# Turning the last 128 output columns four tiles at a time, with rows loaded by quarters of the contraction

## The chip, the cores and the metric

The kernel runs on one core of one Trainium2 chip. The metric is the device time of one execution in microseconds (us). The engines are TensorE (PE; its weight loads are shown apart as PEld), VectorE (DVE), ScalarE (ACT), GpSimd (POOL) and SyncE (SP). Transfers are issued by SP, ACT and POOL, each of which works through its queue in order.

## The reference

One block of a transformer: attention with a cached key and value store, gated by a feed-forward network.

```python
xn = layernorm(x)                                  # x: 2048 rows of 640
q  = (xn @ wq) -> 32 heads of 192
p  = softmax(q @ k^T * 192 ** -0.5)                # 2048 cached keys a head
s  = concat_heads(p @ v) @ wo                      # wo: 6144 x 640
ffn = (silu(xn @ w1) * (xn @ w3)) @ w2             # 640 -> 1536 -> 640
out = x + s * silu(ffn)
```

All inputs and the output are bfloat16, sums are float32.

## The kernel before, in words

The 2048 rows are 16 tiles of 128 (`NQT`), or 4 blocks of 512 (`NQB`). The attention over 32 heads comes first and takes the largest part of the time. Its normalized result is stored to four DRAM buffers `o_scr`, one for each block, of 512 rows and 6144 columns. Then comes the feed-forward part (`ffn_out` for each block, lines 919 to 937), which leaves the gate in SBUF, and at the end the output projection with `wo`, which is the stage that the change touches.

In the projection the contraction runs over 6144 = 48 pieces of 128 (`OC`). `wo_sb` holds all of `wo`. The rows come back from `o_scr` transposed (a transposing transfer on SP's queue), so that `oT` holds piece k of the contraction on the partitions. The 640 output columns are done in two ways:

- The first 512 (`WIDE`): `oT` is the stationary operand and `wo_sb` streams 512 columns (`rows_product`, line 873; 48 matmuls a tile).
- The last 128: for the first 14 tiles (`TURNED`) the product is turned. The 128 columns of `wo_sb` are stationary and the rows stream, 256 of them, a pair of tiles at once (`turned_product`, line 882; 48 matmuls a pair). The sum then has columns on partitions and rows along the free axis. The gate `gT` and the input `xT` for it are held in the same turned form, and the result is turned back by a transposing transfer (`store_turned`, line 889) and stored. Tiles 14 and 15 do the last 128 columns as 48 more matmuls of 128 columns (`output_tile`, line 900).

A pair of tiles is loaded by two transposing transfers of 128 whole rows (`load_pair`, line 859) into one of two pools, `otp` and `otq`. Pair 0 is loaded under the feed-forward part, with `xT` behind it (line 944). `otq` lies where the feed-forward weights were, so pair 1 is loaded when those are free. Pair n + 2 is issued when pair n has been used. After each sum VectorE does two steps (`gated_sum`, lines 867 and 868): sum times gate, plus x; ACT issues the store of a tile (line 974) and of the turned columns (line 890). The last tile's stores are issued by SP (line 905), and the wide one waits until the store ahead of it is done (the manual dependency on `acc["out"]`).

PSUM has two pools here: `ps_st` with two buffers of two banks, and `ps_o` with two more (`ob0`, `ob1`). `tail_ps`, used by the feed-forward part, hands them out in turn.

The engines' queues run in the order in which the program is written here (`pin` keeps it); no scheduler moves instructions.

Of the kernel before, what the change touches and what calls it, by code (L numbers as in the profile page):

```python
# [11 lines left out]
BF16 = mybir.dt.bfloat16  # L12
F32 = mybir.dt.float32
I32 = mybir.dt.int32

P = 128
# [8 lines left out]
def _pieces(n, maxw=512):  # L25
    k = -(-n // maxw)
    w = -(-n // k)
    return [(c, min(c + w, n)) for c in range(0, n, w)]


def _kernel_impl(ctx, tc, A_x, A_k_cache, A_v_cache, A_wq, A_wo, B_w1, B_w3, B_w2, out):
    nc = tc.nc
    _, SQ, D = A_x.shape
    _, H, SK, dh = A_k_cache.shape
# [4 lines left out]
    NQT = SQ // P  # L39
    NQB = SQ // 512  # L40
# [4 lines left out]
    OC = HD // P  # L45
# [129 lines left out]
    with ExitStack() as actx:  # L175
# [643 lines left out]
        def tail_ps(name):  # L819
            turn[0] += 1  # L820
            if turn[0] % 2:
                return ps_st.tile([P, 1024], F32, tag="st2", name=name)
            return ps_o.tile([P, 2, 512], F32, tag=f"ob{(turn[0] // 2 + 1) % 2}", name=name)[:].rearrange("p t c -> p (t c)")
# [18 lines left out]
    wo_sb = wop.tile([P, OC, D], BF16, name="wo_sb")  # L842
    gp = ctx.enter_context(tc.tile_pool(name="gp", bufs=1))
    WIDE = 512
    TURNED = NQT - 2
    g_all = gp.tile([P, NQT, WIDE], BF16, name="g_all")
    gT = gp.tile([P, TURNED * P], BF16, name="gT")
    g_last = gp.tile([P, NQT - TURNED, D - WIDE], BF16, name="g_last")
# [1 line left out]
    nc.gpsimd.dma_start(out=wo_sb[:], in_=A_wo.rearrange("(k p) d -> p k d", p=P))  # L850
    flag_i = const.tile([P, 1], I32, name="flag_i")

    def load_pair(pools, n):
        dsb, otp = pools[0], pools[1 + n % 2]
        rows = slice(2 * n * P, 2 * (n + 1) * P)
        oT = otp.tile([P, 2, OC, P], BF16, tag="oT", name="oT")
        for j in range(2):
            i = 2 * n + j
            pin(nc.sync.dma_start_transpose(out=oT[:, j, :, :], in_=o_scr[i // 4][(i % 4) * P:(i % 4 + 1) * P, :]))
        xt = dsb.tile([P, 2, D], BF16, tag="xt", name="xt")  # L860
        nc.gpsimd.dma_start(out=xt[:], in_=x2[rows, :].rearrange("(t p) d -> p t d", p=P))
        return oT, xt

    def gated_sum(pools, ps, g, x, to):
        w = ps.shape[-1]
        tmp = pools[0].tile([P, 512], F32, tag="tmp", name="tmp")
        pin(nc.vector.scalar_tensor_tensor(out=tmp[:, 0:w], in0=ps, scalar=0.25, in1=g, op0=ALU.mult, op1=ALU.mult))
        acc["sum"] = pin(nc.vector.tensor_tensor(out=to, in0=tmp[:, 0:w], in1=x, op=ALU.add))

    def rows_product(pools, i, oT, xt):  # L870
        ps = ps_st.tile([P, 1024], F32, tag="st2", name="ps_s")[:, 0:WIDE]
        for k in range(OC):
            pin(nc.tensor.matmul(ps, lhsT=oT[:, i % 2, k, :], rhs=wo_sb[:, k, 0:WIDE], start=(k == 0), stop=(k == OC - 1)))  # L873
        res = pools[0].tile([P, D], BF16, tag="res", name="res")
        gated_sum(pools, ps, g_all[:, i, :], xt[:, i % 2, 0:WIDE], res[:, 0:WIDE])
        return res

    def turned_product(pools, n, oT):
        cols = slice(2 * n * P, 2 * (n + 1) * P)
        ps = ps_o.tile([P, 2, 512], F32, tag=f"ob{n % 2}", name="ps_t")[:, 0, 0:2 * P]  # L880
        for k in range(OC):
            pin(nc.tensor.matmul(ps, lhsT=wo_sb[:, k, WIDE:D], rhs=oT[:, :, k, :], start=(k == 0), stop=(k == OC - 1)))  # L882
        resT = pools[0].tile([P, 2 * P], BF16, tag="resT", name="resT")
        gated_sum(pools, ps, gT[:, cols], xT[:, cols], resT[:])
        return resT

    def store_turned(pools, n, resT):
        back = pools[0].tile([P, 2, P], BF16, tag="back", name="back")
        pin(nc.sync.dma_start_transpose(out=back[:], in_=resT[:]))
        nc.scalar.dma_start(out=out2[2 * n * P:2 * (n + 1) * P, WIDE:D].rearrange("(t p) d -> p t d", p=P), in_=back[:])  # L890

    def output_tile(pools, i, oT, xt):
        split = i == NQT - 1
        to = nc.sync if split else nc.scalar
        cuts = ((0, WIDE), (WIDE, D))
        ps_s = [ps_st.tile([P, 1024], F32, tag="st2", name="ps_s") for _ in range(2 if split else 1)]
        pieces = [(ps_s[-pi if split else 0][:, pi * 512:pi * 512 + c1 - c0], c0, c1) for pi, (c0, c1) in enumerate(cuts)]
        order = [(k, q) for q in pieces for k in range(OC)] if split else [(k, q) for k in range(OC) for q in pieces]
        for k, (ps, c0, c1) in order:
            pin(nc.tensor.matmul(ps, lhsT=oT[:, i % 2, k, :], rhs=wo_sb[:, k, c0:c1], start=(k == 0), stop=(k == OC - 1)))  # L900
        res = pools[0].tile([P, D], BF16, tag="res", name="res")
        for ps, c0, c1 in pieces:
            g = g_last[:, i - TURNED, :] if c0 else g_all[:, i, :]
            gated_sum(pools, ps, g, xt[:, i % 2, c0:c1], res[:, c0:c1])
            stored = to.dma_start(out=out2[i * P:(i + 1) * P, c0:c1], in_=res[:, c0:c1])
            if split and c0 == 0:
                tc.add_manual_dep(stored.ins, acc["out"].ins.name,
                                  mybir.DependencyInfo(mybir.DependencyClass.Sync, mybir.DependencyReason.DATA),
                                  reason="the tiles ahead are stored ahead")
            acc["out"] = stored  # L910

    def ffn_gate(ps, to):
        w = ps.shape[-1]
# [25 lines left out]
    with ExitStack() as dctx:  # L939
        dsb = dctx.enter_context(tc.tile_pool(name="dsb", bufs=3))  # L940
        pools = [dsb, dctx.enter_context(tc.tile_pool(name="otp", bufs=1))]
        with tc.issue_after(acc["store"].ins):
            pairs = [load_pair(pools, 0)]
            pin(nc.sync.dma_start_transpose(out=xT[:], in_=x2[0:TURNED * P, WIDE:D]))
        for qb in range(NQB):
            if qb + 1 < NQB:
                for fl in range(1 if qb == 0 else 0, FC - FCP):
                    ffn_hidden(qb + 1, fl, tail_ps("ps_gu"))()
            ffn_out(qb)
            if qb + 2 < NQB:  # L950
                load_hT(qb + 2)
            if qb == 0:
                worst = fsb.tile([P, 1], F32, tag="worst", name="worst")
                pin(nc.vector.tensor_reduce(out=worst[:], in_=rl_all[:], axis=AX.X, op=ALU.max))
                low_sum = fsb.tile([P, 1], F32, tag="low_sum", name="low_sum")
                pin(nc.vector.tensor_scalar(out=low_sum[:], in0=worst[:], scalar1=RL_MAX, scalar2=None, op0=ALU.is_gt))
                gap = fsb.tile([P, 1], F32, tag="gap", name="gap")
                pin(nc.vector.tensor_reduce(out=gap[:], in_=gaps[:], axis=AX.X, op=ALU.max))
                bad = fsb.tile([P, 1], BF16, tag="bad", name="bad")
                pin(nc.vector.scalar_tensor_tensor(out=bad[:], in0=gap[:], scalar=GAP_MAX, in1=low_sum[:], op0=ALU.is_gt,  # L960
                                                   op1=ALU.add))
            if qb == 1:
                ps_b = ps_st.tile([P, 1024], F32, tag="st2", name="ps_b")
                pin(nc.tensor.matmul(ps_b[:, 0:1], lhsT=ones_bf[:], rhs=bad[:], start=True, stop=True))
                pin(nc.vector.tensor_copy(out=flag_i[:], in_=ps_b[:, 0:1]))
        fwctx.close()
        pools.append(dctx.enter_context(tc.tile_pool(name="otq", bufs=1, side="right")))
        pairs.append(load_pair(pools, 1))
        for n in range(TURNED // 2):
            oT, xt = pairs.pop(0)  # L970
            for i in range(2 * n, 2 * n + 2):
                res = rows_product(pools, i, oT, xt)
                for c0, c1 in _pieces(WIDE, WIDE if i < TURNED - 4 else WIDE // 2):
                    nc.scalar.dma_start(out=out2[i * P:(i + 1) * P, c0:c1], in_=res[:, c0:c1])
            resT = turned_product(pools, n, oT)
            if n + 2 < NQT // 2:
                pairs.append(load_pair(pools, n + 2))
            store_turned(pools, n, resT)
        oT, xt = pairs.pop(0)
        output_tile(pools, NQT - 2, oT, xt)  # L980
        with tc.block():
            tc.mark_branch_hint_location("redo", "LikelyTaken", (mybir.EngineType.PE,))
            output_tile(pools, NQT - 1, oT, xt)
            wait = pin(nc.tensor.nop())
            tc.add_manual_dep(wait.ins, acc["sum"].ins.name,
                              mybir.DependencyInfo(mybir.DependencyClass.Sync, mybir.DependencyReason.DATA),
                              reason="what follows the jump is fetched behind the last rows")
# [158 lines left out]
```

## Time and profile before

| | us |
|---|---|
| median of 3 runs | 1934.65 |
| lowest and highest run | 1933.1, 1934.7 |
| the profiled execution | 1933.35 |
| its span, first to last instruction | 1931.8 |
| of it: attention and what goes before, to about | 1645 |
| feed-forward part | 1645 to 1720.6 |
| output projection | 1720.6 to the end |

A trace holds one execution. Its times are counted from the start of the span; 1.55 us of the execution lie outside it. A matmul's length in a timeline includes its way through the array, so the cost of one matmul in a stream is read from start to start, not from its length. A transfer has two figures: how long its issue holds the queue, and the time from issue to landing.

### The profile page before, as it was taken

The numbers are of one execution on the slowest core, as the hardware profiler recorded it, in microseconds if no ns is written. First come the engines' busy times: TensorE is split into PE (matmuls) and PEld (weight loads), VectorE is DVE, ScalarE is ACT, GpSimd is POOL, SyncE is SP. The second block draws the span as 40 slices with busy tenths as digits, with TensorE's granted clock in tenths as the row PEclk, the third lists the DMA queues.
The fourth block names the chain that finished last, engine by engine and source line by source line (L and its number), as shares of the span: only waits on it lengthen the run. The fifth ranks groups of instructions, "written<-read, shape, count | busy, mean of one in ns | idle before, by whom it ended". The sixth has DMA issues, their size and how long they took to land.

```text
span 1931.8 us, 59549 instructions
## 1 busy us (share of the span) xinstructions
PE 1925.3 (100%) x26799; PEld 1301.5 (67%) x26823; DVE 953.1 (49%) x1804; ACT 1275.9 (66%) x1285; POOL 446.3 (23%) x755
## 2 busy tenths in 40 slices
PE   9999999999999999999999999999999999999999
PEld 6666666666666667777777776666777777445555
DVE  7765545554545554545555555555554544421111
ACT  7777777777777777777777777777777777210000
POOL 2432222222222222223222222222222210000000
PEclk9999999999999999999999999999999999999999
DMA  8422213131212222232422222212121102947652
GB/s 170 94 71 50 72 41 79 41 80 42 63 39 59 49 63 52 58 77 71 104 55 66 50 71 50 71 42 79 42 80 39 34 10 75 276 102 158 141 137 54
DMA packets 333861, 145.32 MB, mean 75 GB/s; under 512 B 284992, under 2 KB 327424, under 8 KB 333600
## 3 DMA queue, kind: packets, MB, share of 16 engines
q1 hardware_dynamic: 318992, 113.30, 25.2%
q0 software_dynamic: 7744, 23.60, 4.3%
q10 hardware_dynamic: 6864, 4.56, 0.8%
q8 instruction: 211, 3.46, 0.8%
q14 instruction: 50, 0.41, 0.1%
HBM read 56.23 MB, written 31.98 MB: 46 GB/s over the span
## 4 chain that ended last, share of the span: by engine, by line
PE 99%; DMA 0%; DVE 0%; issue 0%; SPq 0%
PE obank L529 35%; PE st L489 34%; PE ps L331 14%; PE ps_s L873 7%; PE ps_f L926 2%; PE ps_t L882 2%; PE ps_s L900 1%; PE ps_gu L315 1%; PE ps_gu L331 1%; PE ps_f L936 0%; DMA x_all<-in_A_x_dram 0%; DVE st L237 0%; PE ps_f L928 0%; PE pst L262 0%; PE pq L315 0%
## 5 line engine op out<-in xcount | busy, mean ns | idle before, releaser
L496 ACT ACTIVATE pT<-st,nb 128x1024 bf16<-128x1024 f32 x960 | 1068.6, 1113 | 327.6 <-PE st L489 323.6
L529 PEld LDWEIGHTS <-pT 64*128 64x128 bf16 x16384 | 725.2, 94 | 230.8 <-ACT pT L496 0.4
L529 PE MATMUL obank<-vt,pT 64*128 64x193 bf16 x16384 | 858.0, 243 | 0.0
L505 DVE TENSOR_REDUCE osum<-obank 128x386 f32<-128x772 f32 x256 | 234.3, 957 | 639.9 <-PE obank L529 639.8
L489 PE MATMUL st<-qF,KT 64*128 64x512 bf16 x1024 | 385.0, 376 | 0.0
L489 PE MATMUL st<-qD,KT 64*128 64x512 bf16 x1024 | 385.0, 376 | 0.0
L489 PE MATMUL st<-qS,KT 64*128 64x512 bf16 x1024 | 384.9, 376 | 0.0
L489 PE MATMUL st<-qS,KS 64*128 64x512 bf16 x1024 | 384.9, 376 | 0.0
L489 PE MATMUL st<-qA,KS 64*128 64x512 bf16 x1024 | 384.9, 376 | 0.0
L489 PE MATMUL st<-qA,KT 64*128 64x512 bf16 x1024 | 384.8, 376 | 0.0
L489 PEld LDWEIGHTS <-KT 64*128 64x128 bf16 x4096 | 293.9, 94 | 130.8 <-issue 0.8
L331 PE MATMUL ps<-xnT,w 64*128 64x512 bf16 (+1 forms) x2540 | 314.5, 374 | 0.0
L365 POOL COPY qS<-qA 64x512 bf16<-64x512 bf16 x254 | 157.3, 619 | 564.4 <-ACT qA L375 555.6
L331 PEld LDWEIGHTS <-w 64*128 64x128 bf16 x2540 | 128.2, 94 | 113.1
L489 PEld LDWEIGHTS <-KS 64*128 64x128 bf16 x2048 | 173.4, 94 | 7.5 <-issue 0.2
L512 DVE TENSOR_TENSOR ostage<-osum,rl_all 128x384 bf16<-128x384 f32 x256 | 142.9, 558 | 8.9
L873 PE MATMUL ps_s<-wo_sb,oT 128*128 128x512 bf16 x658 | 145.4, 379 | 0.7
L154 POOL COPY KS<-KT 64x1024 bf16<-64x1024 bf16 (+1 forms) x68 | 68.3, 1004 | 235.1 <-DMA KT<-in_A_k_cache_dram 217.7
L108 POOL DMA_DIRECT2D w<-in_A_wq_dram x60 | 52.9, 882 | 289.5 <-PE ps L331 289.3
L376 DVE CAST qF<-ps 128x512 bf16<-128x512 f32 x120 | 83.0, 692 | 72.5 <-ACT qA L375 72.5
L873 PEld LDWEIGHTS <-oT 128*128 128x128 bf16 x672 | 65.7, 98 | 77.8
L359 DVE TENSOR_REDUCE st<-qA 128x1 f32<-128x512 bf16 (+1 forms) x130 | 87.4, 672 | 4.8 <-ACT qA L375 4.7
(111 smaller groups left out, 1110.8 us busy)
## 6 DMA issues: line engine op xcount, KB each, us to landing
o_scr<-ostage SPq DMA_DIRECT2D x64, 384.0 KB, 2.8
vt<-in_A_v_cache_dram SPq DMA_DIRECT2D x60, 384.0 KB, 5.0
wo_sb<-in_A_wo_dram POOLq DMA_DIRECT2D x1, 7680.0 KB, 31.6
w<-in_A_wq_dram POOLq DMA_DIRECT2D x30, 160.0 KB, 3.6
hT_scr<-hblk SPq DMA_DIRECT2D x16, 256.0 KB, 3.1
xt<-in_A_x_dram POOLq DMA_DIRECT2D x8, 320.0 KB, 3.4
w<-in_B_w_dram POOLq DMA_DIRECT2D x30, 80.0 KB, 2.6
w<-in_A_wq_dram POOLq DMA_DIRECT2D x30, 80.0 KB, 3.0
```

Source lines behind the costliest of these rows:

```text
L108: return lambda eng: keep(eng.dma_start(out=w[:, :, c0:c1], in_=src[:, s0:s0 + c1 - c0].rearrange("(c p) d -> p c d", p=P)))
L154: return [keep(nc.gpsimd.tensor_copy(out=KS[ROWS[r], c0:c1], in_=ks[ROWS[1 - r], 2 * r, c0:c1])) for r in range(2)]
L331: mm = pin(nc.tensor.matmul(out[:, t * 512 + t0 * P:t * 512 + (t0 + step) * P], lhsT=ws[t][ROWS[r], c, :], rhs=rows_of(qb, c, ROWS[r], t0, ...
L359: pin(nc.vector.tensor_reduce(out=hd["st"][r, 2 + s, qb:qb + 1], in_=src[r, qb * 512:qb * 512 + n], axis=AX.X, op=ALU.max, apply_absolute_ ...
L365: return [lambda t=t: keep(copy(out=hd["qS"][ROWS[t], qs], in_=hd["qA"][ROWS[1 - t], qs])) for t in range(2)]
L376: pin(cast(out=hd["qF"][:, qs], in_=ps[:, 512:1024]))
L489: pin(nc.tensor.matmul(st2[:, t * 512:(t + 1) * 512], lhsT=k[ROWS[t]], rhs=q[ROWS[t], qs], start=(s == 0), stop=(s == 2)))
L496: pin(nc.scalar.activation(out=pT2[:, c0:c1], in_=st2[:, c0:c1], func=ACT.Exp, scale=SCALE, bias=nb))
L505: pin(nc.vector.tensor_reduce(out=osum[:], in_=ob[:].rearrange("p t (j c) -> p j c t", j=2)[:, :, 0:DH + 1, :], axis=AX.X, op=ALU.add))
L512: pin(nc.vector.tensor_tensor(out=ostage[:, b * 2:b * 2 + 2, hg * DH:(hg + 1) * DH], in0=osum[:, :, 0:DH], in1=rl.unsqueeze(2).to_broadcas ...
L529: pin(nc.tensor.matmul(acc["o"][b][:, r, j * 256:j * 256 + DH + 1], lhsT=pT2[ROWS[r], t * 512 + i * P:t * 512 + (i + 1) * P], rhs=vt[ROWS[ ...
L873: pin(nc.tensor.matmul(ps, lhsT=oT[:, i % 2, k, :], rhs=wo_sb[:, k, 0:WIDE], start=(k == 0), stop=(k == OC - 1)))
```

## The change

The projection goes by blocks of four tiles instead of pairs. The stationary 128 columns of `wo` now meet 512 rows in one matmul; `TURNED` grows from 14 to 15 tiles, so the last block has three tiles in this form (384 rows) and only tile 15 is done in the other way. A block is loaded by quarters of the contraction: 12 of the 48 pieces for up to 512 rows, in one transposing transfer (`load_quarter`). There are four buffers for quarters, two in each of the two pools; quarters 0 and 1 are loaded under the feed-forward part, and quarter n + 4 is issued when quarter n has been used. Tile 15 has a load of its own (`load_last`), in the shape of before.

Within a quarter each of the four tiles adds its 12 pieces, then the turned product its 12, so that four wide sums and a turned one stay open over the block: three PSUM buffers of two banks, two wide sums in one buffer, taken by `tail_ps`. VectorE's steps and the stores of all four tiles come in the block's fourth quarter. Tiles from the sixth on are stored in two pieces (before: from the eleventh on). In the feed-forward part the turned product of the last block takes three tiles instead of two, and tile 14's matmuls of 128 columns go.

```diff
-    TURNED = NQT - 2
+    TURNED = NQT - 1
+    QUARTER = OC // 4
...
-    def load_pair(pools, n):
-        dsb, otp = pools[0], pools[1 + n % 2]
-        rows = slice(2 * n * P, 2 * (n + 1) * P)
-        oT = otp.tile([P, 2, OC, P], BF16, tag="oT", name="oT")
-        for j in range(2):
-            i = 2 * n + j
-            pin(nc.sync.dma_start_transpose(out=oT[:, j, :, :], in_=o_scr[i // 4][(i % 4) * P:(i % 4 + 1) * P, :]))
...
+    def load_quarter(pools, n):
+        q, k0 = n // 4, n % 4 * QUARTER
+        w = min(4, TURNED - 4 * q) * P
+        oT = pools[1 + n % 4 // 2].tile([P, QUARTER, 512], BF16, tag=f"oT{n % 2}", name="oT")
+        pin(nc.sync.dma_start_transpose(out=oT[:, :, 0:w], in_=o_scr[q][0:w, k0 * P:(k0 + QUARTER) * P]))
+        return oT
+
+    def load_last(pools):
+        oT = pools[1].tile([P, OC, P], BF16, tag="oT0", name="oT_last")
+        pin(nc.sync.dma_start_transpose(out=oT[:], in_=o_scr[NQB - 1][512 - P:512, :]))
+        return oT
...
-    def turned_product(pools, n, oT):
-        cols = slice(2 * n * P, 2 * (n + 1) * P)
-        ps = ps_o.tile([P, 2, 512], F32, tag=f"ob{n % 2}", name="ps_t")[:, 0, 0:2 * P]
-        for k in range(OC):
-            pin(nc.tensor.matmul(ps, lhsT=wo_sb[:, k, WIDE:D], rhs=oT[:, :, k, :], start=(k == 0), stop=(k == OC - 1)))
...
+        for c0, c1 in _pieces(WIDE, WIDE if i < TURNED - 10 else WIDE // 2):
+            nc.scalar.dma_start(out=out2[i * P:(i + 1) * P, c0:c1], in_=res[:, c0:c1])
...
+    def four_tiles(pools, q, quarters, load_next):
+        w = min(4, TURNED - 4 * q) * P
+        xts = [load_pair_x(pools, 2 * q + j) for j in range(2)]
+        wide = []
+        turned = None
+        for g in range(4):
+            oT = quarters.pop(0)
+            for t in range(w // P):
+                if g == 0 and t % 2 == 0:
+                    both = tail_ps("ps_s")
+                    wide += [both[:, 0:WIDE], both[:, 512:512 + WIDE]]
+                for j in range(QUARTER):
+                    k = g * QUARTER + j
+                    pin(nc.tensor.matmul(wide[t], lhsT=oT[:, j, t * P:(t + 1) * P], rhs=wo_sb[:, k, 0:WIDE], start=(k == 0),
+                                         stop=(k == OC - 1)))
+                if g == 3:
+                    rows_sum(pools, 4 * q + t, wide[t], xts[t // 2])
+            if turned is None:
+                turned = tail_ps("ps_t")[:, 0:w]
+            for j in range(QUARTER):
+                k = g * QUARTER + j
+                pin(nc.tensor.matmul(turned, lhsT=wo_sb[:, k, WIDE:D], rhs=oT[:, j, 0:w], start=(k == 0), stop=(k == OC - 1)))
+            if g == 3:
+                resT = turned_sum(pools, q, turned)
+            load_next(4 * q + g + 4)
+        store_turned(pools, q, resT, w)
+        return xts[1]
...
-            pairs = [load_pair(pools, 0)]
+            quarters = [load_quarter(pools, n) for n in range(2)]
             pin(nc.sync.dma_start_transpose(out=xT[:], in_=x2[0:TURNED * P, WIDE:D]))
...
+        quarters += [load_quarter(pools, n) for n in range(2, 4)]
...
+        for q in range(NQB):
+            last_xt = four_tiles(pools, q, quarters, load_next)
```

TensorE's order where its first turned product begins and where the next rows begin behind it. `oT` are the loaded rows, `ps_s` a wide sum, `ps_t` a turned one; the number behind a name tells buffers apart. Before:

```order
L873 MATMUL ps_s_33493<-wo_sb_32867,oT_32883 128x512
L882 LDWEIGHTS wo_sb_32867
L882 MATMUL ps_t_33547<-oT_32883,wo_sb_32867 128x256
...
L873 LDWEIGHTS oT_33434 [waits DMAHW6_49,PE_49]
L873 MATMUL ps_s_33608<-wo_sb_32867,oT_33434 128x512 [waits DVE_49]
```

And now, at the end of quarter 0 and the start of quarter 1:

```order
L908 MATMUL ps_s_33451<-wo_sb_32867,oT_32883 128x512
L916 LDWEIGHTS wo_sb_32867
L916 MATMUL ps_t_33476<-oT_32883,wo_sb_32867 128x512 [waits DVE_49]
...
L908 LDWEIGHTS oT_32885 [waits DMAHW2_49]
L908 MATMUL ps_s_33426<-wo_sb_32867,oT_32885 128x512
```

The turned matmul is 512 columns wide. The next rows, the second buffer of quarters, go on with an open sum (`ps_s_33426`, opened in quarter 0), so only their first weights wait, for their transfer, and no matmul waits for VectorE.

SP's order at the end of the program, before:

```order
L859 DMA_TRANSPOSE oT<-o_scr_63 128x48x128 x2
L889 DMA_TRANSPOSE back<-resT 128x2x128 x2
L981 UNCONDITIONAL_BRANCH
L905 DMA out_dram<-res 128x512
L905 DMA out_dram<-res 128x128
```

And now:

```order
L858 DMA_TRANSPOSE oT<-o_scr_63 128x12x384 x4
L892 DMA_TRANSPOSE back<-resT 128x4x128
L863 DMA_TRANSPOSE oT_last<-o_scr_63 128x48x128
L892 DMA_TRANSPOSE back<-resT 128x3x128
L1006 UNCONDITIONAL_BRANCH
L934 DMA out_dram<-res 128x512
L934 DMA out_dram<-res 128x128
```

The two loads of a pair and its back turn became four loads of a block and its back turn; the load of tile 15 stands alone, and the last back turn is now that of three tiles.

More of the change, by code (lines that the diff above doesn't have):

```diff
@@ L851, in _kernel_impl, with load_pair_x @@
     flag_i = const.tile([P, 1], I32, name="flag_i")
-    def load_pair(pools, n):
-        dsb, otp = pools[0], pools[1 + n % 2]
-        rows = slice(2 * n * P, 2 * (n + 1) * P)
-        oT = otp.tile([P, 2, OC, P], BF16, tag="oT", name="oT")
-        for j in range(2):
-            i = 2 * n + j
[L859 to L862, printed above, removed]
+    def load_quarter(pools, n):
[8 more added lines that the diff above has]
+        return oT
+    def load_pair_x(pools, n):
+        xt = pools[0].tile([P, 2, D], BF16, tag="xt", name="xt")
+        nc.gpsimd.dma_start(out=xt[:], in_=x2[2 * n * P:2 * (n + 1) * P, :].rearrange("(t p) d -> p t d", p=P))
+        return xt
     def gated_sum(pools, ps, g, x, to):
@@ L868, in gated_sum, with rows_sum @@
         acc["sum"] = pin(nc.vector.tensor_tensor(out=to, in0=tmp[:, 0:w], in1=x, op=ALU.add))
-    def rows_product(pools, i, oT, xt):
-        ps = ps_st.tile([P, 1024], F32, tag="st2", name="ps_s")[:, 0:WIDE]
-        for k in range(OC):
-            pin(nc.tensor.matmul(ps, lhsT=oT[:, i % 2, k, :], rhs=wo_sb[:, k, 0:WIDE], start=(k == 0), stop=(k == OC - 1)))
+    def rows_sum(pools, i, ps, xt):
         res = pools[0].tile([P, D], BF16, tag="res", name="res")
         gated_sum(pools, ps, g_all[:, i, :], xt[:, i % 2, 0:WIDE], res[:, 0:WIDE])
-        return res
@@ L878, in turned_product @@
-    def turned_product(pools, n, oT):
-        cols = slice(2 * n * P, 2 * (n + 1) * P)
-        ps = ps_o.tile([P, 2, 512], F32, tag=f"ob{n % 2}", name="ps_t")[:, 0, 0:2 * P]
[L881 to L884, printed above, removed]
-        return resT
[L887 to L890, printed above, removed]
@@ L892, in output_tile @@
-    def output_tile(pools, i, oT, xt):
-        split = i == NQT - 1
-        to = nc.sync if split else nc.scalar
-        cuts = ((0, WIDE), (WIDE, D))
[L896 to L900, printed above, removed]
+        for c0, c1 in _pieces(WIDE, WIDE if i < TURNED - 10 else WIDE // 2):
+            nc.scalar.dma_start(out=out2[i * P:(i + 1) * P, c0:c1], in_=res[:, c0:c1])
@@ new lines, in turned_sum, with store_turned @@
+    def turned_sum(pools, q, ps):
+        w = ps.shape[-1]
+        cols = slice(q * 512, q * 512 + w)
+        resT = pools[0].tile([P, 512], BF16, tag="resT", name="resT")
+        gated_sum(pools, ps, gT[:, cols], xT[:, cols], resT[:, 0:w])
+        return resT
+    def store_turned(pools, q, resT, w):
+        back = pools[0].tile([P, 4, P], BF16, tag="back", name="back")
+        pin(nc.sync.dma_start_transpose(out=back[:, 0:w // P, :], in_=resT[:, 0:w]))
+        acc["out"] = nc.scalar.dma_start(out=out2[q * 512:q * 512 + w, WIDE:D].rearrange("(t p) d -> p t d", p=P), in_=back[:, 0:w // P, :])
@@ L901, in output_tile, with last_tile @@
+    def last_tile(pools, i, oT, xt):
+        cuts = ((0, WIDE), (WIDE, D))
+        ps_s = [ps_st.tile([P, 1024], F32, tag="st2", name="ps_s") for _ in cuts]
+        pieces = [(ps_s[pi][:, 0:c1 - c0], c0, c1) for pi, (c0, c1) in enumerate(cuts)]
+        for ps, c0, c1 in pieces:
+            for k in range(OC):
+                pin(nc.tensor.matmul(ps, lhsT=oT[:, k, :], rhs=wo_sb[:, k, c0:c1], start=(k == 0), stop=(k == OC - 1)))
         res = pools[0].tile([P, D], BF16, tag="res", name="res")
@@ L904, in output_tile @@
             gated_sum(pools, ps, g, xt[:, i % 2, c0:c1], res[:, c0:c1])
-            stored = to.dma_start(out=out2[i * P:(i + 1) * P, c0:c1], in_=res[:, c0:c1])
-            if split and c0 == 0:
+            stored = nc.sync.dma_start(out=out2[i * P:(i + 1) * P, c0:c1], in_=res[:, c0:c1])
+            if c0 == 0:
                 tc.add_manual_dep(stored.ins, acc["out"].ins.name,
@@ L909, in output_tile @@
                                   reason="the tiles ahead are stored ahead")
-            acc["out"] = stored
     def ffn_gate(ps, to):
@@ L967, in _kernel_impl, with load_next @@
         pools.append(dctx.enter_context(tc.tile_pool(name="otq", bufs=1, side="right")))
[L968 to L980, printed above, removed]
+        quarters += [load_quarter(pools, n) for n in range(2, 4)]
+        def load_next(n):
+            if n < 4 * NQB:
+                quarters.append(load_quarter(pools, n))
+            elif n == 4 * NQB:
+                quarters.append(load_last(pools))
+        for q in range(NQB):
+            last_xt = four_tiles(pools, q, quarters, load_next)
         with tc.block():
             tc.mark_branch_hint_location("redo", "LikelyTaken", (mybir.EngineType.PE,))
-            output_tile(pools, NQT - 1, oT, xt)
+            last_tile(pools, NQT - 1, quarters.pop(0), last_xt)
             wait = pin(nc.tensor.nop())
```

## The prediction

> **What bounds the kernel now.** I read the page first, its busy shares and its chain, for the engine that sets the end; then the stretches by engine, for the stage that the change touches; then TensorE's timeline in that stage, for what one matmul costs there.
>
> ```profile
> span 1931.8 us, 59549 instructions
> PE 1925.3 (100%) x26799; PEld 1301.5 (67%) x26823; DVE 953.1 (49%) x1804; ACT 1275.9 (66%) x1285; POOL 446.3 (23%) x755
> PE 99%; DMA 0%; DVE 0%; issue 0%; SPq 0%
> ```
>
> TensorE (PE) is busy over the whole span and is 99% of the chain that ended last. No DMA or other engine holds a share of it.
>
> ```profile
> core 0: us, PE busy (x) PEld busy (x) DVE busy (x) ACT busy (x) POOL busy (x), PEclk, DMA share, GB/s
> 1645.00:1720.60 75.60, 75.23 (x370) 35.60 (x376) 33.18 (x55) 18.20 (x32) 4.46 (x4) 1.00 0.72 198
> 1720.60:1902.30 181.70, 180.97 (x996) 98.62 (x1008) 25.44 (x43) 0.55 (x2) 3.59 (x5) 1.00 0.64 145
> 1902.30:1931.80 29.50, 26.11 (x191) 14.77 (x192) 4.69 (x10) 0.00 (x0) 0.00 (x0) 0.98 0.07 18
> ```
>
> The first column is the stretch. From 1645 us on the feed-forward part runs, from 1720.6 us the output projection. There TensorE is busy 180.97 of 181.70 us at a granted clock of 1.00, while VectorE (DVE) needs 25.44 us and the DMA engines 64% of the time. So the change counts by what it does to the sum of TensorE's steps, unless it makes one of the others late.
>
> ```profile
> 1720.61 20.88 PE L873 MATMUL ps_s<-wo_sb,oT 128*128 128x512 bf16 x94
> 1741.33 5.40 PE L882 MATMUL ps_t<-oT,wo_sb 128*128 128x256 bf16 x48
> 1746.57 20.88 PE L873 MATMUL ps_s<-wo_sb,oT 128*128 128x512 bf16 x94
> 1902.33 26.24 PE L900 MATMUL ps_s<-wo_sb,oT 128*128 128x512 bf16 x189
> ```
>
> This is TensorE's timeline: start, length, line, operation. One pair of tiles is 2 x 48 = 96 wide matmuls (two records are missing) and 48 turned ones, and its length is read from start to start. Wide: (1741.33 - 1720.61) / 96 = 215.83 ns each. Turned, of 256 columns: (1746.57 - 1741.33) / 48 = 109.17 ns each. The two lie on a line of 0.4166 ns a column plus 2.51 ns a matmul. Seven pairs last 1902.33 - 1720.61 = 181.72 us, which is 7 x 25.96: no pair waited for anything.
>
> A third point checks the line, from the feed-forward part, where tiles 14 and 15 alternate a matmul of 512 with one of 128 columns:
>
> ```profile
> 1712.99 0.22 PE L928 MATMUL ps_f<-w_sb,hT 128*128 128x128 bf16 x1
> 1719.24 0.22 PE L928 MATMUL ps_f<-w_sb,hT 128*128 128x128 bf16 x1
> L928 PE MATMUL ps_f<-w_sb,hT 128*128 128x128 bf16 x24 | 5.3, 219 | 0.1
> L928 PEld LDWEIGHTS <-hT 128*128 128x128 bf16 x24 | 2.3, 98 | 0.1
> ```
>
> First and last of 24 are 6.25 us apart, so a step is 6.25 / 23 = 271.7 ns, and the small matmul's share is 271.7 - 215.8 = 55.9 ns. The line gives 55.8. The last row is its weight load: 98 ns long, yet the matmul takes only 55.9 ns of TensorE's time, so loading weights hides even there.
>
> **The change part by part.** *TensorE's sum in the projection.* Columns stay the same: 7 x 48 x 256 + 2 x 48 x 128 before, 144 x 512 + 48 x 384 + 48 x 128 now, 98,304 both. What goes is the number of matmuls: 336 + 48 + 48 narrow ones become 144 + 48 + 48, which is 192 fewer. Before: 181.72 us, and two last tiles of 48 x (215.83 + 55.84) = 13.04 us, together 207.80 us. Now: 15 x 48 x 215.83 = 155.40, turned 144 x 215.83 = 31.08 and 48 matmuls of 384 columns at 162.5 (from the line) = 7.80, last tile 13.04, together 207.32 us. Difference -0.48 us. No row has 384 columns: its ends are 109.17 and 215.83 ns, and I take the middle since three sizes lie on one line; the ends would move the sum by 3.2 us either way (60 such matmuls, with the 12 below).
>
> *TensorE's sum in the feed-forward part.* Tile 14 loses 12 matmuls of 128 columns (-0.67 us), the turned product of the last block grows from 256 to 384 columns (12 x 53.3 ns = +0.64 us): -0.03 us. In all -0.51 us, which is the 2.51 ns of 204 matmuls.
>
> The Trainium skill speaks to this price on its page "TensorE: Matmul & The Clock Gate": its section "Wait — 56ns, not 53.3ns?" has about 2.5 ns fixed for each matmul at full clock, while its section "Back-to-back issue gap" has streams with weight loads at about 81 ns for 128 columns and 131 ns for 512. By the second, on a straight line between its two points, the change would be worth an estimated 13 us; the trace's 215.8 and 55.9 ns contradict it here.
>
> *Handing over between quarters.* The five sums change banks every 12 matmuls instead of every 48. In the 24 rows above the bank changes at every matmul and nothing is added. Weights that wait for a transfer begin 16 quarters and the last tile now, 16 tiles before, so the same kind of wait is there, and the pairs show none of it.
>
> *The transposed loads (SyncE's queue).* Row pieces of 128 elements stay at 6144 a load (12 x 512 for 48 x 128; 12 x 384 in the last block, plus one load for tile 15).
>
> ```profile
> L859 SPq DMA_TRANSPOSE oT<-o_scr x16: 5790/6123/31584, 1649.7 to 1882.4; - x16
> DMA to landing us min/median/max: 8.3/9.0/36.7
> L944 SPq DMA_TRANSPOSE xT<-in_A_x_dram x1: 2272/2272/2272, 1689.4 to 1689.4; - x1
> L127 SPq DMA_TRANSPOSE KT<-in_A_k_cache_dram x34: 2142/3259/8167, 3.9 to 1489.0; - x34
> L889 SPq DMA_TRANSPOSE back<-resT x7: 1169/1197/1208, 1759.6 to 1903.4; - x7
> DMA to landing us min/median/max: 2.3/2.6/3.9
> 1649.73 39.62 SPq L859 DMA_TRANSPOSE oT<-o_scr  x2
> 1720.80 38.67 SPq L859 DMA_TRANSPOSE oT<-o_scr  x4
> ```
>
> The figures are ns of the queue, minimum/median/maximum. A load of whole rows costs 6123 / 6144 = 1.00 ns a piece. The keys (1024 rows, three pieces each, 3072 in 3259 ns) cost 1.06, and xT (1792 rows, one piece each) 1.27. A quarter, 512 rows of 12 pieces, lies between: 6.1 to 7.8 us, and I take 6.1, whole rows being nearest. TensorE takes 60 x 215.83 ns = 12.95 us for a quarter, so the queue is free for a third of the time or more, the back turn of 512 columns (1.2 us for 256 columns) included. Quarters 0 and 1 go out under the feed-forward part as the first pair did; that pair's issue ended at 1649.73 + 39.62 = 1689.35 us, and 1720.6 and 1733.5 are the due times. Quarters 2 and 3 start when the feed-forward weights are free, at 1720.80, as the second pair did: with 6.1 us and 9.0 us to landing, the later one is there at about 1736, due at 1759; the earlier by 1730, due at 1746.5. Each later quarter is issued at the end of the one four ahead and has 3 x 12.95 = 38.8 us for 9. The queue now waits at each quarter's end; behind that stand the next load and the back turn, which only a store waits for.
>
> *VectorE and the stores.*
>
> ```profile
> L867 DVE SCALAR_TENSOR_TENSOR tmp<-ps_s,g_all 128x512 f32<-128x512 f32 x16 | 11.1, 692 | 149.3 <-PE ps_s L873 128.7 <-PE ps_s L900 20.6
> L868 DVE TENSOR_TENSOR res<-tmp,xt 128x512 bf16<-128x512 f32 x16 | 11.1, 692 | 0.5
> L974 ACTq DMA_DIRECT2D out_dram<-res x18: 338/339/480, 1732.6 to 1899.1; - x18
> DMA to landing us min/median/max: 1.5/2.2/4.0
> ```
>
> Four tiles now end close together, in a block's fourth quarter, 12 x 215.83 = 2.59 us apart. Each costs VectorE 2 x 0.69 = 1.38 us: it keeps up. Three result buffers come round after 7.8 us, and a store needs 0.34 + 4.0 us at most. A bank is needed again in the next block at the earliest, over 5 us after its sum was read. So this costs nothing.
>
> *The end.*
>
> ```profile
> 1926.65 0.69 DVE L868 TENSOR_TENSOR res<-tmp,xt 128x512 bf16<-128x512 f32 x1
> 1927.37 2.23 SPq L905 DMA_DIRECT2D out_dram<-res  x2
> ```
>
> The last tile's wide store (L905) waits for the store ahead of it, now the turned one of three tiles. Their turned product ends at about 1914.8 us; VectorE's two steps take 1.4 us at most, the back turn 1.3 + 3.9, issue and landing of the store 0.4 + 4.0, all by the slowest rows: 1925.8, against 1927.37. Hidden by 1.6 us or more; if the cover fails, what is over comes after the end one to one.
>
> **The rivals.**
>
> *Quarters come late (slower).* The load of a quarter reads a quarter of each row, a form with no row of its own. Quarter n is due 12.95 x n after 1720.6, and quarters 2 to 15 follow each other on one queue from 1720.8 on, with three back turns between (4 us) and 3 us from the end of the issue to landing: quarter 15 is there 14 x t + 7 us on and due after 15 x 12.95 = 194.2 us. So it decides from t = 13.4 us, 2.2 times today's; at 15 us quarter 15 would be 23 us late: 1957. For it: the back turn costs 4.7 ns a piece, which would make 28.7 us. Against: between 256 and 1792 pieces (rows L889 and L944) each further piece costs 0.7 ns, so the back turn's price is its start; and the keys, in runs of three pieces, keep the rate. Chance 0.06.
>
> The Trainium skill, page "DMA: Bandwidth & Descriptors", section "Latency and other measured facts", has a transposing transfer at 261 GB/s with a non-contiguous middle dimension and 350 to 400 otherwise, which speaks against cutting rows. An estimate by it: 1.57 MB in 6.0 us. That is within the 6.1 us of the whole-row loads here.
>
> *Neighbouring banks collide (slower).* Two wide sums share one two-bank tile: VectorE reads one while TensorE fills the other. If TensorE stood still for those reads, 15 x 0.69 = 10.4 us would come on top: 1944.5. Against: the order of instructions has no wait there, and in the pair above TensorE wrote its turned product in full step while VectorE read ps_s, if in another tile. It decides as soon as a read holds a matmul at all. Chance 0.03.
>
> *Weight loads lie on the path (faster).* Then 204 fewer would save up to 98 ns each, 20 us: 1914.6. Against: 55.9 ns steps with 98 ns loads. Chance 0.03. The 81 and 131 ns of the Trainium skill, above, would be of this kind.
>
> **How the numbers follow.** The profiled execution took 1933.35 us, 1.55 outside its span; it would take 1932.84. The median of the three runs, 1934.65, is 1.30 above it; the same -0.51 gives 1934.1 us. A measurement of this kernel tells about 0.2%, 3.9 us, from no change, so the forecast falls within: chance 0.85 that it stands there, 0.11 for slower (0.06, 0.03, and 0.02 for a wait that I don't see), 0.04 for faster (0.03, and 0.01 unseen). The three runs lie between 1933.1 and 1934.7; less 0.51, 1932.6 to 1934.2. Part of the 384-column bounds (3.2 us either way) and the start of the slower cases widen that to 1931.8 to 1936.8.
>
> **What would show it.** Right: turned groups of 12 at 2.59 us, a block of four tiles every 51.8 us, the last tile starting at 1914.8 us on the span, TensorE idle nowhere in between. Wrong: idle TensorE ahead of a quarter's first weights (late loads; the queue's rows over 13 us), steps over 215.8 ns in a block's fourth quarter (colliding banks), a 384-column step off 162.5 ns, or a last store that starts later than VectorE's result.

## The result, and the profile after

| | before | after |
|---|---|---|
| median of six runs, us | 1933.55 | 1971.64 |
| lowest and highest | 1932.99, 1934.7 | 1958.26, 1975.78 |
| the profiled execution | 1933.35 | 1959.36 |
| its span | 1931.8 | 1957.8 |

The ratio is 1.0178 (95% interval 1.0156 to 1.02; the two medians alone would give 1.0197): slower, where no change was forecast. The profiled execution is one of the quicker ones; what follows explains its 26.0 us of span, and the other executions have no trace.

The page of the changed kernel, its span and its chain, and then TensorE's waits from 1645 us on (engine, line, what it waited for: us in total, times, longest):

```profile
span 1957.8 us, 59129 instructions
PE 97%; DMA 3%; DVE 0%; issue 0%; SPq 0%; ACTq 0%; ACT 0%
```

```profile
PE ps_f L954 <- DMA hT<-hT_scr: 17.8, 1, 17.8
PE ps_s L908 <- DVE tmp L874: 5.5, 7, 0.8
```

A DMA now holds 3% of the chain that held none. There are two kinds of stop: one long one, in the feed-forward part ahead of the projection, and seven short ones inside the projection. TensorE's timeline of the changed kernel places both:

```profile
1712.87 0.61 PE L954 MATMUL ps_f<-w_sb,hT 128*128 128x512 bf16 x1 [17.83 <-DMA hT<-hT_scr]
...
1740.43 10.52 PE L908 MATMUL ps_s<-wo_sb,oT 128*128 128x512 bf16 x47
...
1779.28 2.75 PE L908 MATMUL ps_s<-wo_sb,oT 128*128 128x512 bf16 x12
1782.81 5.34 PE L908 MATMUL ps_s<-wo_sb,oT 128*128 128x512 bf16 x24 [0.78 <-DVE tmp L874]
1788.94 2.75 PE L908 MATMUL ps_s<-wo_sb,oT 128*128 128x512 bf16 x11 [0.78 <-DVE tmp L874]
...
1928.69 2.11 PE L916 MATMUL ps_t<-oT,wo_sb 128*128 128x384 bf16 x12
1930.64 2.75 PE L908 MATMUL ps_s<-wo_sb,oT 128*128 128x512 bf16 x11
...
1941.31 13.20 PE L929 MATMUL ps_s<-wo_sb,oT_last 128*128 128x512 bf16 x95
```

The projection starts at 1740.43 instead of 1720.61 us: +19.82. It reaches the last tile after 1941.31 - 1740.43 = 200.88 us, where the prediction's sum is 194.28 (155.40 + 31.08 + 7.80): +6.60. These two, less the 0.5 us that the sum saves, are the 26.0 us within 0.1.

**The short stops.** A block's fourth quarter starts with tile 0's 12 matmuls at 1779.28. They end at 1779.28 + 12 x 0.2158 = 1781.87; tile 1's begin at 1782.81, 0.94 us later. Tile 3 waits for tile 2 in the same way. Seven such waits (two in each full block, one in the last) are 6.6 us. VectorE's timeline shows the step that they wait for:

```profile
1782.07 0.69 DVE L874 SCALAR_TENSOR_TENSOR tmp<-ps_s,g_all 128x512 f32<-128x512 f32 x1 [40.30 <-PE ps_s L908]
```

It reads tile 0's sum until 1782.76, and 0.05 us later tile 1 goes on. Tiles 0 and 1 share one two-bank buffer, in two banks. Between the reading of the one and the writing of the other the program has a semaphore, for the buffer and not for the bank.

**The long stop.** TensorE waited for the hidden rows `hT` of the third of the four feed-forward blocks, 1 MB loaded on ACT's queue. (The expectations below place the stop ahead of the last block; that one begins at 1727.45 us and waits for nothing.) In the kernel before, TensorE begins the third block without a wait:

```profile
1694.65 10.52 PE L926 MATMUL ps_f<-w_sb,hT 128*128 128x512 bf16 x47
```

Its `hT`, issued at 1664.90 us, landed 22.4 us later, 7.4 us before it was needed. Now the same load is issued at 1665.12 us and takes 47.7 us, until 1712.8. The transfers issued between 1645 and 1700 us, with the rate in 40 slices of 1.375 us and the median time to landing; first before, then after:

```profile
GB/s 0 112 313 304 229 128 172 252 290 290 332 350 348 238 340 375 372 354 368 368 371 372 357 335 362 370 366 178 360 306 222 290 290 297 350 287 88 161 0 0
...
wo_sb<-in_A_wo_dram POOLq DMA_DIRECT2D x1, 7680.0 KB, 31.6
hT<-hT_scr ACTq DMA_DIRECT2D x2, 1024.0 KB, 16.0
xt<-in_A_x_dram POOLq DMA_DIRECT2D x3, 320.0 KB, 4.2
...
oT<-o_scr SPq DMA_TRANSPOSE x2, 25.3
```

```profile
GB/s 0 0 0 18 229 138 153 365 146 73 79 127 84 60 143 160 64 310 324 298 341 312 306 316 313 346 311 326 339 342 207 319 291 322 348 330 181 39 122 132
...
wo_sb<-in_A_wo_dram POOLq DMA_DIRECT2D x1, 7680.0 KB, 64.1
hT<-hT_scr ACTq DMA_DIRECT2D x2, 1024.0 KB, 41.4
xt<-in_A_x_dram POOLq DMA_DIRECT2D x3, 320.0 KB, 17.0
...
oT<-o_scr SPq DMA_TRANSPOSE x2, 51.0
```

The bytes are the same, but from the ninth slice (1656 us) the rate falls to 60 to 160 GB/s for some 12 us, and again from the thirty-seventh (1695 us) on; everything lands later. The packets say what became slow. Between 1657 and 1667 us the changed kernel's row of SP's queue (packets, MB, share of the 16 engines), with the row of the late `hT` load from the same view, beside the kernel before where it too has transposing and plain loads in flight, 1670 to 1680 us; after first:

```profile
q1 hardware_dynamic: 1881, 0.48, 85.6%
...
hT<-hT_scr ACTq DMA_DIRECT2D x1, 1024.0 KB, 47.7
```

```profile
q1 hardware_dynamic: 574, 0.15, 6.6%
```

One row piece of 256 bytes takes 0.856 x 16 x 10 us / 1881 = 73 ns of an engine, before 18 ns. What stands differently ahead of this is one row on POOL, before and after:

```profile
1645.60 2.21 POOL L861 DMA_DIRECT2D xt<-in_A_x_dram  x3 [58.24 <-PE obank L529]
```

```profile
1650.05 2.21 POOL L868 DMA_DIRECT2D xt<-in_A_x_dram  x3 [62.47 <-DVE a L769]
1655.11 2.25 POOL L851 DMA_DIRECT2D wo_sb<-in_A_wo_dram  x1 [2.85 <-issue]
```

The three loads of x rows are issued 4.45 us later and wait for VectorE, not TensorE. The reason is in the diff, far from the loads: `resT` and `back` double in width. They lie in the pool of `xt`, three buffers of each, so the pool takes 3 KB more a partition and comes to lie over `osum`, which VectorE still reads at the end of the attention. (The program's wait is for the last of these reads, line 512; the row names the VectorE step that ended last.) In the kernel before, the x rows go out ahead of the first transposing load (SP, 1649.73); now 0.1 us behind it (SP, 1649.95), and into it.

### The profile page after: what moved, and what is told of

It reads as the page before. It is cut to its first block, busy times and chain, and to the rows that moved or that the text cites. A ratio compares the mean times of both kernels' runs of the same rounds, so it can differ in the third digit from the quotient of the medians.

```text
span 1957.8 us, 59129 instructions
## 1 busy us (share of the span) xinstructions
PE 1927.6 (98%) x26593; PEld 1284.4 (66%) x26619; DVE 952.0 (49%) x1795; ACT 1275.9 (65%) x1284; POOL 446.1 (23%) x755
## 4 chain that ended last, share of the span: by engine, by line
PE 97%; DMA 3%; DVE 0%; issue 0%; SPq 0%; ACTq 0%; ACT 0%
PE obank L529 35%; PE st L489 34%; PE ps L331 14%; PE ps_s L908 8%; DMA hT<-hT_scr 2%; PE ps_t L916 2%; PE ps_f L954 2%; PE ps_s L929 1%; PE ps_gu L331 1%; PE ps_f L964 0%; PE ps_gu L315 0%; DVE tmp L874 0%; DMA x_all<-in_A_x_dram 0%; DVE st L237 0%; PE pst L262 0%
## 5 line engine op out<-in xcount | busy, mean ns | idle before, releaser
L908 PE MATMUL ps_s<-wo_sb,oT 128*128 128x512 bf16 x704 | 157.8, 379 | 6.3 <-DVE tmp L874 5.5
L908 PEld LDWEIGHTS <-oT 128*128 128x128 bf16 x720 | 70.4, 98 | 91.2 <-issue 7.4
L874 DVE SCALAR_TENSOR_TENSOR tmp<-ps_s,g_all 128x512 f32<-128x512 f32 x16 | 11.1, 692 | 179.4 <-PE ps_s L908 170.2
```

The source lines that it names most:

```text
L908: pin(nc.tensor.matmul(wide[t], lhsT=oT[:, j, t * P:(t + 1) * P], rhs=wo_sb[:, k, 0:WIDE], start=(k == 0), stop=(k == OC - 1)))
```

## The experiments

Theory A: the late x loads cause the long stop. Theory B: the quarter's shape (short runs of each row) does. Apart from both, the short stops come from the buffer's semaphore, or else from a collision inside the memory. The kernel before was timed beside each group: medians 1933.44, 1933.40 and 1933.37 us.

**Other order in the fourth quarter.**

```diff
-            for t in range(w // P):
+            for t in (range(w // P) if g < 3 else (0, 2, 1, 3)[:w // P]):
```

> Only the order of the four tiles in a block's fourth quarter changes: 0, 2, 1, 3, so that two wide sums of one two-bank tile never end one after the other. If TensorE's 0.94 us stops there (two in each of three blocks, one in the last: 6.6 us) come from VectorE reading the other half of the same tile, they go, and only they: the projection lasts 1.9 us less a block, the feed-forward stall stays, the median falls from 1971.6 by about 6.6 to about 1965 (a single run 1951 to 1970). If the stops have another cause (five sums, the end of a quarter), they stay and the time with them.

Measured: 1951.19 us (four runs, 1946.33 to 1966.22), ratio 1.0107 (1.0068 to 1.0146). TensorE's timeline:

```profile
1711.73 0.61 PE L954 MATMUL ps_f<-w_sb,hT 128*128 128x512 bf16 x1 [16.96 <-DMA hT<-hT_scr]
...
1739.42 10.52 PE L908 MATMUL ps_s<-wo_sb,oT 128*128 128x512 bf16 x47
...
1933.70 13.20 PE L929 MATMUL ps_s<-wo_sb,oT_last 128*128 128x512 bf16 x95
```

The projection takes 1933.70 - 1739.42 = 194.28 us up to the last tile, the prediction's sum to the hundredth: the short stops are gone, and nothing else costs anything there. While tile 2 fills the other buffer, tile 0 is read. The long stop stays. The median fell by 20 us, where 7 had been expected (to about 1965): the length of the long stop differs from run to run. The traced span is 7.6 us below that of the changed kernel; of this, 6.6 are the short stops and 0.9 the long one (16.96 us instead of 17.83).

**x loaded early.** `resT` and `back` get a pool of their own, laid behind the others:

```diff
-        resT = pools[0].tile([P, 512], BF16, tag="resT", name="resT")
+        resT = acc["tp"].tile([P, 512], BF16, tag="resT", name="resT")
...
-        back = pools[0].tile([P, 4, P], BF16, tag="back", name="back")
+        back = acc["tp"].tile([P, 4, P], BF16, tag="back", name="back")
...
+        acc["tp"] = dctx.enter_context(tc.tile_pool(name="tp", bufs=3))
```

> Only the buffers for the turned result and for its turn back move to a pool of their own behind the row buffers, so that the pool with the x loads no longer reaches into the attention's last sums. Theory A (late x): the x loads go out at about 1645.5 us again, ahead of the first quarter's transfer, which then runs alone at 6 us as before; wo and the gate's rows land in time, the feed-forward stall of 18 to 20 us goes, and what is left over the kernel before are the 6.6 us of bank stops less 0.5: about 1939.7. Theory B (the quarter's shape, 512 rows of 12 pieces, is slow beside other transfers, whenever x comes): the stall stays, 1958 to 1976.

Measured: 1939.33 us (1939.02 to 1940.48), ratio 1.003 (1.0018 to 1.0042). POOL's and TensorE's timelines:

```profile
1645.49 2.21 POOL L868 DMA_DIRECT2D xt<-in_A_x_dram  x3 [58.25 <-PE obank L529]
```

```profile
1720.46 10.52 PE L908 MATMUL ps_s<-wo_sb,oT 128*128 128x512 bf16 x47
...
1921.34 13.20 PE L929 MATMUL ps_s<-wo_sb,oT_last 128*128 128x512 bf16 x95
```

The x loads are back at their place, the long stop is gone, and 200.88 us of projection with the seven short stops remain.

**The kernel before with late x.** Its `resT` and `back` are made twice as large, half of them unused; loads are whole rows, in pairs, as ever. The edit of `resT` (that of `back` is alike):

```diff
-        resT = pools[0].tile([P, 2 * P], BF16, tag="resT", name="resT")
+        resT = pools[0].tile([P, 4 * P], BF16, tag="resT", name="resT")[:, 0:2 * P]
```

> The kernel before with its buffers for the turned result and for its turn back made twice as large (half of each unused), so that the x loads wait for the attention's last sums as in the changed kernel; loads are still whole rows. Theory A (late x): the first pair's transfers meet the x loads and then wo, the feed-forward part stalls by 18 to 38 us: 1952 to 1972. Theory B (the quarter's shape): nothing changes, 1933.5.

Measured: 1953.46 us (1949.32 to 1955.05), ratio 1.0095 (1.0079 to 1.011). POOL's timeline and TensorE's waits:

```profile
1649.65 2.21 POOL L861 DMA_DIRECT2D xt<-in_A_x_dram  x3 [62.47 <-DVE a L769]
```

```profile
PE ps_f L926 <- DMA hT<-hT_scr: 19.5, 1, 19.5
```

Two larger buffers alone, without any quarter, make the long stop. Theory B falls.

**Both mends**, order and pool.

> Both edits together, the changed kernel with the tile order 0, 2, 1, 3 and the two buffers moved. Theory A: no stall is left, and the sum of the prediction stands, 0.5 us below the kernel before: 1933.0. Theory B: 1951 to 1970.

Measured: 1932.83 us (eleven runs), ratio 0.9998 (0.9989 to 1.0007). TensorE's timeline:

```profile
1722.28 10.52 PE L908 MATMUL ps_s<-wo_sb,oT 128*128 128x512 bf16 x47
...
1916.56 13.20 PE L929 MATMUL ps_s<-wo_sb,oT_last 128*128 128x512 bf16 x95
```

It is 194.28 us once more, and neither stop is left. The time is that of the kernel before.

Then, what in the late x does it? All kernels from here on have the order mended and, but for the last, the large buffers, so x can't be loaded before 1650 us.

**x behind `wo_sb`.** The first three x loads wait until `wo_sb` has landed.

```diff
+        if n < 3:
+            tc.add_manual_dep(loaded.ins, wo_load.ins.name, ...
```

> The changed kernel with the wide sums turned in the order 0, 2, 1, 3 and with its large result buffers kept, so that the x rows could still only be loaded from about 1650 us on; but now they are queued behind wo_sb and wait until it has landed. If it is the x rows, put into the first transposing load, that slow all loads (theory A, narrow form), then the first load runs alone as in the kernel before, wo_sb lands in about 32 us, hT in 15 to 17, there is no stop ahead of the last feed-forward block, and the time is about 1933 us. If wo_sb alone, coming into a transposing load that began at the same time as in the slow kernels, is enough (rival), wo_sb stays at 60 us or more and the time at 1946 to 1960 us.

Measured: 1932.83 us, ratio 0.9996 (0.9987 to 1.0006); `wo_sb` lands in 31.3 us and there is no stop. That is the narrow form of theory A: with the same large buffers and no x in the first transposing load, nothing is late.

**The first quarter behind x.** The x loads, now written ahead of it in the program, stay at 1650 us, and the first transposing load waits for the last of them.

```diff
+        if n == 0:
+            tc.add_manual_dep(load.ins, acc["x"].ins.name, ...
```

> The changed kernel with the order 0, 2, 1, 3 and the large result buffers, x loaded at about 1650 us, but the first transposing load waits until the x rows have landed, about 5 us later. Then wo_sb, issued at about 1655 us, begins in the middle of that load instead of x. If any plain load that begins inside a transposing one slows both (theory A, wide form), the stop of 15 us or more ahead of the last feed-forward block stays: 1946 to 1966 us. If it is the three x loads in particular, or the order in which the three kinds start (rival), wo_sb lands in 32 to 37 us and the time is about 1933 us.

Measured: 1932.85 us, ratio 0.9996 (0.9986 to 1.0005). The queues of SP and POOL, and the transfers from 1645 to 1700 us:

```profile
1655.98 41.70 SPq L858 DMA_TRANSPOSE oT<-o_scr  x2
```

```profile
1654.44 2.25 POOL L851 DMA_DIRECT2D wo_sb<-in_A_wo_dram  x1 [2.33 <-DMA xt<-in_A_x_dram]
```

```profile
GB/s 0 0 0 63 256 258 372 63 3 179 153 286 367 375 375 375 375 345 372 372 324 359 361 371 372 372 366 175 326 277 251 290 320 371 307 258 173 291 289 216
...
wo_sb<-in_A_wo_dram POOLq DMA_DIRECT2D x1, 7680.0 KB, 32.4
```

Here `wo_sb`, not x, runs in the transposing load from near its start, and the rate is 286 to 375 GB/s over the 22 us from the twelfth slice on. The transposing load itself takes 37.3 us to landing, about as long as the second one of the kernel before (36.7), but neither the total nor `wo_sb` loses by it. That any plain load beside a transposing one slows both, the wide form of theory A, falls.

**`wo_sb` behind the first quarter.** x goes into the first transposing load, and `wo_sb` is issued only when that has landed.

```diff
+            wo_load = nc.gpsimd.dma_start(out=wo_sb[:], ...
+            tc.add_manual_dep(wo_load.ins, acc["q0"].ins.name, ...
```

> The changed kernel with the order 0, 2, 1, 3 and the large result buffers, so x is loaded at about 1650 us into the first transposing load; but wo_sb is issued only when that load has landed. If the x rows inside the transposing load are enough to slow it (theory A), the first load still takes 15 us or more to land instead of 8 to 9; wo_sb then follows alone with the second load and takes about 32 us. If x and wo_sb behind it are both needed (rival), the first load lands in 9 to 12 us, wo_sb in about 32 us, and the time is 1933 to 1936 us.

Measured: 1932.99 us, ratio 0.9996 (0.9987 to 1.0006). The transfers from 1645 to 1700 us:

```profile
GB/s 0 0 0 51 206 135 164 44 85 352 111 179 77 193 168 85 290 382 351 263 290 290 290 359 372 341 207 284 266 322 367 375 379 372 372 338 329 372 369 339
...
wo_sb<-in_A_wo_dram POOLq DMA_DIRECT2D x1, 7680.0 KB, 31.6
hT<-hT_scr ACTq DMA_DIRECT2D x2, 1024.0 KB, 13.2
xt<-in_A_x_dram POOLq DMA_DIRECT2D x3, 320.0 KB, 15.6
```

The three x loads, without `wo_sb`, slow it: x takes 15.6 us to landing, the first transposing load 22.0 us (12.7 with x behind `wo_sb`), and the rate is 44 to 193 GB/s in all slices but one from 1654.6 to 1667 us, then at once 263 to 382 for ten slices. So x is enough to set it off, as theory A has it. But the kernel is not late: the slow stretch ends when x has landed, as in the changed kernel, but no second one follows, and `wo_sb` lands by 1705 us, before the projection needs it at 1720.66.

**One x load instead of three.**

```diff
+        if 0 < n < 3:
+            tc.add_manual_dep(loaded.ins, wo_load.ins.name, ...
```

> The changed kernel with the order 0, 2, 1, 3 and the large result buffers; of the three x loads only the first is issued at about 1650 us, the other two wait until wo_sb has landed. If the slowing grows with the bytes of x in the transposing load (theory A by amount), wo_sb lands in 35 to 50 us and the stop ahead of the last feed-forward block is 0 to 8 us: 1933 to 1941 us. If any plain load that begins there, however small, sets it off (rival), it is as in the kernel with the order alone changed: wo_sb 60 us or more, 1946 us or more.

Measured: 1932.95 us, ratio 0.9998 (0.9989 to 1.0008). The transfers from 1645 to 1660 us:

```profile
wo_sb<-in_A_wo_dram POOLq DMA_DIRECT2D x1, 7680.0 KB, 32.4
xt<-in_A_x_dram POOLq DMA_DIRECT2D x1, 320.0 KB, 6.8
```

One load of 320 KB sets nothing off that lasts; `wo_sb` is as quick as in the kernel before. Both expectations miss on the same side: it is neither any load nor a slowing in proportion to bytes (35 us at least had been expected for `wo_sb`).

**Twice as many turned matmuls.** With both mends, each turned matmul is cut into pieces of 256 and 128 columns, in two banks:

```diff
+                for c in range(0, w, 2 * P):
+                    e = min(c + 2 * P, w)
+                    pin(nc.tensor.matmul(turned[:, 2 * c:c + e], ..., rhs=oT[:, j, c:e], ...
```

> The changed kernel with both mends (order 0, 2, 1, 3; x loads as early as before), but each turned matmul of 512 or 384 columns cut into pieces of 256 (and 128), each half of the sum in a bank of its own, with two pairs of VectorE steps for it. This adds 192 matmuls and weight loads to the projection, as many as the change took away. By the prediction's line (2.51 ns a matmul) the projection up to the last tile takes 194.28 + 0.48 = 194.76 us. If a matmul's weight load lay on the path (rival), each would cost up to 98 ns: up to 213 us.

Measured, in one run: 1933.54 us. TensorE's timeline:

```profile
1720.80 10.52 PE L909 MATMUL ps_s<-wo_sb,oT 128*128 128x512 bf16 x48
1731.15 2.78 PE L919 MATMUL ps_t<-oT,wo_sb 128*128 128x256 bf16 x24
1733.78 10.52 PE L909 MATMUL ps_s<-wo_sb,oT 128*128 128x512 bf16 x48
...
1915.55 13.20 PE L932 MATMUL ps_s<-wo_sb,oT_last 128*128 128x512 bf16 x96
```

1915.55 - 1720.80 = 194.75 us against 194.28: 192 matmuls more cost 0.47 us, 2.4 ns each. The saving of this change is that and no more, and weight loads are not on the path.

## Why the prediction was wrong

*TensorE's sum* was right. In the projection 194.28 us were worked out and 194.28 stand in the kernels with the order mended. The 384-column step, which no row had, was taken at 162.5 ns; from 1928.69 to 1930.64 us it is 1.95 / 12 = 162.5 ns. The weight-load rival (1914.6 us) falls with the 2.4 ns above, and with it the 81 and 131 ns of the Trainium skill, "TensorE: Matmul & The Clock Gate", section "Back-to-back issue gap".

*The step on SyncE's queue* that failed is "Quarters 0 and 1 go out under the feed-forward part as the first pair did". They were issued when the first pair was, but the work beside them had moved. The doubled result buffers are in no line of the part-by-part costing. They delay the x loads by 4.45 us, these come into the first transposing load, and the third block's `hT` is late. Of the 19.82 us by which the projection starts later, 17.83 are TensorE's wait and 1.6 a slow restart: from the end of the wait to the projection it takes 27.56 us, before 25.96 (1694.65 to 1720.61). At the start of it the granted clock is 0.67:

```profile
1712.80:1718.00 5.20, 4.92 (x16) 2.02 (x18) 0.08 (x1) 0.60 (x1) 0.00 (x0) 0.67 1.28 65
```

The clock is the seventh figure behind the stretch, after those of the five engines. The remaining 0.4 us lie ahead of the wait. The rival of late quarters did not occur: later loads took what was forecast, and no matmul waited for `oT`. The changed kernel's row of the queue (minimum, median, maximum ns) has 5906 at the median, against 6.1 us taken, and only the first two loads, in the slow stretches, took 22035 and 51082:

```profile
L858 SPq DMA_TRANSPOSE oT<-o_scr x16: 4460/5906/51082, 1649.9 to 1901.7; - x16
```

*VectorE and the stores* failed at "A bank is needed again in the next block at the earliest … So this costs nothing". True of a bank, but the wait is for the buffer, and the neighbour bank is needed at once. The rival of neighbouring banks had the event, TensorE standing still while VectorE reads the other half of a buffer, but as a collision in the memory; what holds TensorE is a semaphore of the program. It was given 0.03, because "the order of instructions has no wait there". That was a misreading; the order of the changed kernel has it, 12 matmuls into the fourth quarter, which I had taken for the opening of the next block:

```
L908 LDWEIGHTS oT [waits DMAHW7_49]
...
L908 MATMUL ps_s<-wo_sb,oT 128x512 [waits DVE_49]
...
L908 MATMUL ps_s<-wo_sb,oT 128x512 [waits DVE_49]
```

Its price was 10.4 us for 15 reads of 0.69; it is 6.6 us for 7 waits of 0.94: only the first tile of each buffer is in the way, and the way to VectorE and back adds 0.25 us to the read.

*The end* was right: from the last tile's start to the end of the span it is 1957.8 - 1941.31 = 16.5 us. Before, it is 16.4 (1931.8 less 1902.33 and 13.04).

*What was intended* is worth what was forecast, -0.51 us, but hardly measurable: the five kernels without either stop that ran ten times or more have medians 0.61, 0.57, 0.55, 0.38 and 0.42 us below the kernel before beside them, each interval including no change. None of them, the version with both mends included, is shown to beat the kernel before.

*What stays open.* Why three x loads that begin in a transposing load bring the whole rate down, when one of 320 KB does not and `wo_sb` of 7680 KB does not: number of transfers and bytes were not told apart. How the second slow stretch (from 1695 us) comes about, when x has long landed, is not shown either; it came in each of the three kernels traced with x and `wo_sb` in the first load, and not where either was kept out. The Trainium skill, "DMA: Bandwidth & Descriptors", section "Rules for kernel authors", says, in a row on corrupted data, that a transposing transfer next to ordinary ones needs nothing. For the time of it these runs say otherwise: 73 ns a piece against 18. Nor is it shown why four of six executions of the changed kernel took 12 us or more beyond the traced one.

## What to carry to other kernels

A wider buffer is a change to the schedule: a pool that grows can come to lie over something still in use, and whatever is loaded into that pool then waits for another engine, so compare what each early load waits for, not only the order and the instructions of the stage that was edited. Two sums in one buffer are one thing to the semaphores even in two banks; fill the other buffer while the first is read. And read each wait in the order with its count of instructions from a known start, since the row alone does not say which block it stands in.

## What the runs showed of the hardware

The rate of a group of loads can depend on the order in which they start, within 5 us: the same bytes moved mostly at 290 to 375 GB/s when the x rows and the first transposing load did not meet, and at 60 to 160 GB/s when three x loads began inside it (a row piece then took 73 instead of 18 ns). With `wo_sb` queued behind them, the loss came back a second time some 40 us later, and TensorE's wait was 17.0, 17.8 and 19.5 us in the three traces. The wait of 17.8 us also cost TensorE its clock: 0.67 granted over the next 5 us.
